# Second products of four experts with the model's columns on the partitions, turned back through memory

## The chip, the cores and the metric

The kernel runs on one core of a Trainium2 chip. The metric is the device time of one execution in microseconds (us), shown as the median of three runs.

## What is computed

The program is a linear-recurrence attention followed by a mixture of eight experts with the best two experts for each token. Only the experts matter here. For N = 3072 tokens of D = 384 numbers, E = 8 experts and F = 1024 hidden columns:

```python
out = np.zeros((N, D), dtype=np.float32)
for e in range(E):
    for k in range(2):
        mask = top2[:, k] == e
        h = np.maximum(x[mask] @ w1[e], 0.0)
        out[mask] += top2_w[mask, k, None] * (h @ w2[e])
```

## The kernel before, in words

The tokens of an expert lie in a table in memory, with room for up to 832 of them. Experts 2 to 7 are taken in the order of their token counts (`rank`, `EX`), so each position in the loop at L1193 has a fixed number of rows: `REST` (L347) gives 64, 64, 64, 48, 32, 16, 16 and 0 for positions 0 to 7. "Expert e" below is the e-th in this order. Its rows come in two pieces. The first piece (`w == 0`) has 256 + REST[e] rows, in row tiles 0, 1 (128 rows each) and 2 (REST[e] rows). The second piece (`w == 1`) has 512 rows, in tiles 3 to 6.

Every float32 factor is split into two parts, a high part and the remainder (`split`, `h`, `x`), and every product is the sum of three: high times high, high times low, low times high. TensorE therefore does three matmuls for each block.

An expert is worked off in this order (L1197 to L1216):

- `load_w2` (L841): four DMAs on SP's queue bring the second weights into the three buffers `raw`; ScalarE casts the high part (L829), VectorE subtracts for the low part (L830).
- `gather_o` (L904): GpSimd gathers the rows of `out` that belong to the expert's tokens into the tiles `ao`.
- `mm1` (L883) for both pieces: for each of eight blocks f of hidden columns, nine matmuls of 128 stationary columns (of W1) and n moving columns (the tokens), into one of four PSUM banks `ph`. ScalarE applies the ReLU (L898), VectorE forms the low part (L901). In the first piece VectorE does that in two instructions, since the remainder's rows are laid out apart, beside a padded gap that GpSimd clears (L892).
- in between, SP loads the next expert's tokens (`load_x`) and first weights (`load_w1`). `x_P` (L789) splits the tokens' 32-bit words into two planes of 16 bits (ScalarE, L794) in the tiles `xp0` and `xp1` and writes them to memory, and `x_L` (L798) reads them back with twelve transposing DMAs (L803).
- `mm2` (L914) for the first piece: for each full row tile 24 matmuls with 128 columns of h stationary and the 384 columns of W2 moving, into one of two banks `po`. For tile 2, eight matmuls whose stationary operand holds high and low rows side by side (L927) and eight more (L930); ScalarE copies the low half out (L933) and VectorE adds it (L934). After each tile VectorE adds the gated result to `ao` (L935, `kept`) and GpSimd scatters `ao` into `out` (L936).
- `mm2` for the second piece, tile by tile, and after the tiles the planes of the next expert are put together (`x_T`, L865): VectorE copies the planes into one tile `xj` (L877), which has a single buffer, ScalarE casts (L880), VectorE subtracts (L881). A manual edge keeps each such copy behind the last `kept` before it.

What orders the work: the engines run their queues in order. Up to the end of expert 1 the order is written out by hand (`ORDER`). From expert 2 on a planner fills each engine's queue. It prefers what stands earlier in the program, and takes a later instruction when the earlier one isn't ready by its own reckoning. On SP a callback (`queue`, L1186) chains all DMAs of this loop in program order:

```python
    def queue(ins):
        if ENG.get(ins.engine) == "SP" and not type(ins).__name__.startswith(("Bass", "InstRegister")):
            if loads:
                tc.add_manual_dep(ins, loads[-1].name, after, reason="order")
            loads.append(ins)
```

Of the kernel before, what the change touches and what calls it, by code (L numbers as in the profile page):

```python
# [9 lines left out]
F32 = mybir.dt.float32  # L10
# [3 lines left out]
U16 = mybir.dt.uint16  # L14
I32 = mybir.dt.int32
AF = mybir.ActivationFunctionType
OP = mybir.AluOpType
# [302 lines left out]
def kernel(  # L320
# [8 lines left out]
    nc = tc.nc  # L329
# [5 lines left out]
    N, DM = out.shape  # L335
    E = w_gate.shape[1]
    FF = w1.shape[2]
    KD = DM // 128
    KF = FF // 128
# [6 lines left out]
    G0 = 3  # L346
    REST = (64, 64, 64, 48, 32, 16, 16, 0)  # L347
    JS = ((0, 1, 2), (3, 4, 5, 6))
    TO = (0, 128, 256, 0, 128, 256, 384)

    def width(e, w):
        return 256 + REST[e] if w == 0 else 512

    def tile_rows(e, j):
        return REST[e] if j == 2 else 128

    def tiles_of(e, w):
        return [j for j in JS[w] if tile_rows(e, j)]

    def pad(e):  # L360
        return -(-REST[e] // 32) * 32
# [3 lines left out]
    xs = nc.dram_tensor("xs", [E * N, ROW], F32, kind="Internal").ap()  # L365
    es = nc.dram_tensor("es", [NT, HD], F32, kind="Internal").ap()
    xp = nc.dram_tensor("xp", [2, 7 * 128, 2 * DM], U16, kind="Internal").ap()
    xd = nc.dram_tensor("xd", [N, DM + E], F32, kind="Internal").ap()

    cp = ctx.enter_context(tc.tile_pool(name="cp", bufs=1))  # L370
# [39 lines left out]
    none = cp.tile([128, ROW], F32, name="none")  # L410
# [14 lines left out]
    ap = ctx.enter_context(ExitStack())  # L425
# [361 lines left out]
    after = mybir.DependencyInfo(mybir.DependencyClass.NoSync, mybir.DependencyReason.DATA)  # L787

    def x_P(e, w):  # L789
        js = JS[w]  # L790
        src_t = (xga, xgb)[w]
# [6 lines left out]
    def x_L(e, w):  # L798
        lo, n = JS[w][0] * 128, width(e, w)
        for kk in range(KD):  # L800
# [11 lines left out]
    W1, W2, XW, HT, GW, OX = {}, {}, {}, {}, {}, {}  # L812
    where = {}

    def mt(shape, dt, name, **kw):

        return where.setdefault(name, mpools[-1]).tile(shape, dt, name=name, **kw)
# [9 lines left out]
    order = mybir.DependencyInfo(mybir.DependencyClass.NoSync, mybir.DependencyReason.DATA)  # L827
# [13 lines left out]
    def load_w2(e):  # L841
        for f2 in range(KF // 2):
            r = mt([128, FF], F32, name="raw", bufs=RAW)
            rv = r[:, :2 * DM].rearrange("p (f d) -> p f d", f=2)
            nc.sync.dma_start(rv, of(w2, e)[f2 * 256:(f2 + 1) * 256, :].rearrange("(f p) d -> p f d", p=128))
            W2[f2] = [mt([128, 2, DM], F32R, name=f"w2{x}{f2}") for x in "hl"]
            split(rv, *W2[f2])
# [17 lines left out]
    def x_T(e, w, kk):  # L865
        n = width(e, w)
        src_t = xga if w == 0 else xgb
        js = JS[w]
        x = XW[w, kk] = mt([128, 2, width(0, w)], F32R, name=f"x{w}{kk}")[:, :, 0:n]
        if e < 2:  # L870
            p = ps_tile("px")
            for j in js:
                o = TO[j]
                nc.tensor.transpose(p[:, o:o + 128], src_t[:, j - js[0], kk * 128:(kk + 1) * 128], ident)
        else:
            p = mt([128, 512], F32, name="xj")
            t = nc.vector.tensor_copy(p[:, :n].bitcast(U16).rearrange("p (d two) -> p two d", two=2), XU[w, kk])  # L877
            if e > 2:
                tc.add_manual_dep(t.ins, kept[-1].ins.name, after, reason="order")
        nc.scalar.copy(x[:, 0, :], p[:, :n])  # L880
        nc.vector.tensor_tensor(x[:, 1, :], p[:, :n], x[:, 0, :].bitcast(F32), op=OP.subtract)  # L881

    def mm1(e, w, fs=range(KF)):  # L883
        n = width(e, w)
        for f in fs:

            h = mt([128, 2 * width(0, w)], F32R, name=f"h{w}{f}")
            t, u = (REST[e], pad(e)) if w == 0 else (0, 0)
            m = n - t + u
            HT[w, f] = h[:, 0:m + t], h[:, m + t:]  # L890
            if u > t:
                nc.gpsimd.memset(h[:, n:m].bitcast(F32), 0.0)  # L892
            p = ps_tile("ph", 4)
            ms = [(i, j, kk) for kk in range(KD) for i, j in ((0, 0), (0, 1), (1, 0))]
            for c, (i, j, kk) in enumerate(ms):
                nc.tensor.matmul(p[:, :n], W1[e, kk][i][:, f * 128:(f + 1) * 128], XW[w, kk][:, j, :],  # L896
                                 start=(c == 0), stop=(c == len(ms) - 1))
            nc.scalar.activation(h[:, 0:n], p[:, :n], AF.Relu)  # L898
            for dst, a, b in ((m + t, 0, n - t), (m, n - t, n)):
                if a < b:  # L900
                    nc.vector.scalar_tensor_tensor(h[:, dst:dst + b - a], p[:, a:b], 0.0, h[:, a:b].bitcast(F32),  # L901
                                                   op0=OP.max, op1=OP.subtract)

    def gather_o(e):  # L904
        for j in tiles_of(e, 0) + tiles_of(e, 1):
            w = tile_rows(e, j)
            nc.gpsimd.indirect_dma_start(  # L907
                out=ao[j][0:w, :], out_offset=None, in_=out,
                in_offset=bass.IndirectOffsetOnAxis(ap=OX[e][0:w, j:j + 1], axis=0),
                bounds_check=N - 1, oob_is_err=False)  # L910

    osc, kept = {}, []

    def mm2(e, w, js=None):  # L914
        for j in js or tiles_of(e, w):
            n, o, u = tile_rows(e, j), TO[j], pad(e)
            p = psO.tile([128, 512], F32, name="po")
            a, g = ao[j][0:n, :], GW[e][0:n, j:j + 1]
            if n == 128:
                ms = [(f, i, k2) for f in range(KF) for i, k2 in ((0, 0), (0, 1), (1, 0))]  # L920
                for m, (f, i, k2) in enumerate(ms):
                    nc.tensor.matmul(p[:, :DM], HT[w, f][i][:, o:o + 128], W2[f // 2][k2][:, f % 2, :],  # L922
                                     start=(m == 0), stop=(m == len(ms) - 1))
            else:

                for f in range(KF):
                    nc.tensor.matmul(p[0:u + n, :DM], HT[w, f][0][:, o:o + u + n], W2[f // 2][0][:, f % 2, :],  # L927
                                     start=(f == 0), stop=(f == KF - 1), skip_group_check=True)
                for f in range(KF):
                    nc.tensor.matmul(p[0:n, :DM], HT[w, f][0][:, o:o + n], W2[f // 2][1][:, f % 2, :],  # L930
                                     start=False, stop=(f == KF - 1), skip_group_check=True)
                lo = mt([64, DM], F32, name="lo")[0:n]
                nc.scalar.copy(lo, p[u:u + n, :DM])  # L933
                nc.vector.scalar_tensor_tensor(a, lo, g, a, op0=OP.mult, op1=OP.add)  # L934
            kept.append(nc.vector.scalar_tensor_tensor(a, p[0:n, :DM], g, a, op0=OP.mult, op1=OP.add))  # L935
            d = nc.gpsimd.indirect_dma_start(  # L936
                out=out, out_offset=bass.IndirectOffsetOnAxis(ap=OX[e][0:n, j:j + 1], axis=0),
                in_=a, in_offset=None, bounds_check=N - 1, oob_is_err=False)
            for x in osc.setdefault(e, []):
                tc.declare_no_dep(d.ins, x.ins, reason="tokens differ")  # L940
            osc[e].append(d)


    P = dict(la=10, p1=7, d1=1, p2=6, dt=0, ds=0, lqk=6, p3=4, d3=0, q=2, lv=4, xu=0.5, ss=3, gl=0, gd=0.25,
             tr=1.4, sc=-0.2, st=0.05, y=0.2, up=0.4, w1=18, w2=21.1, xt=18.5, m1=19.1, dm=0.26, xu1=22.8, w1b=23, co=6, hg=50,
# [2 lines left out]
    for g in range(NG):  # L948
        f = B * g + .5
        q1, q2, q3 = P.get(f"s{g}", (P["p1"], P["p2"], P["p3"]))  # L950
        for j in range(B // 2):
            m = B * g // 2 + j
            h = phase_of(m) // 2
            i = [x for x in range(m + 1) if phase_of(x) == 2 * h].index(m)
# [6 lines left out]
        for j in range(B):  # L961
            n = B * g + j
# [123 lines left out]
    psO = mctx.enter_context(tc.tile_pool(name="psO", bufs=2, space=PSUM, reuse_waits="tile"))  # L1086
    psB.append(mctx.enter_context(tc.tile_pool(name="psB", bufs=2, space=PSUM, reuse_waits="tile")))
    ao = [mp.tile([128, DM], F32, name=f"ao{j}") for j in range(7)]
# [49 lines left out]
    for e, tokens in ORDER.items():  # L1138
        tokens = tokens.split()
# [53 lines left out]
    for e in range(2, E):  # L1193
        if e == 3:
            flag = flags()
            held.close()
        load_w2(e)  # L1197
        gather_o(e)
        mm1(e, 0)
        if e + 1 < E:  # L1200
            load_x(e + 1, 0, xga)
            load_x(e + 1, 1, xgb)
        mm1(e, 1)
        if e + 1 < E:
            load_w1(e + 1)
            for w in range(2):
                x_G(e + 1, w)
                x_P(e + 1, w)
            for w in range(2):
                x_L(e + 1, w)  # L1210
        mm2(e, 0)
        for j in JS[1]:
            mm2(e, 1, (j,))
            if e + 1 < E:
                for w, kk in {3: ((0, 0), (0, 1)), 4: ((0, 2), (1, 0)), 5: ((1, 1),), 6: ((1, 2),)}[j]:
                    x_T(e + 1, w, kk)  # L1216
    nc.pop_inst_callback()
    mctx.close()

# [168 lines left out]
```

## Time and profile before

| what | value |
|---|---|
| median of 3 runs | 675.37 us (674.38 to 676.07) |
| the profiled execution's own time | 675.33 us |
| its span, first to last instruction | 673.6 us |
| TensorE busy | 655.4 us (97%) |
| VectorE, ScalarE, GpSimd busy | 433.4, 357.6, 181.6 us |
| mean granted TensorE clock | 0.997 of full speed |

The profiled execution took 1.7 us more than its span, and 0.04 us less than the median. Experts 3 to 7 fill the last 272 us of it. Busy shares are means over the whole span, so what a change to one stage is worth has to be read from that stage's rows.

### The profile page before, as it was taken

To read this page: it belongs to the slowest core of one execution; us is meant where nothing else is said; L and a number is where in the kernel's file an instruction comes from. 1 tells how busy PE (TensorE), PEld (TensorE's weight loads), DVE (VectorE), ACT (ScalarE), POOL (GpSimd) and SP (SyncE) were. 2 spreads that over 40 slices of the span, in tenths; PEclk is the share of its full clock that TensorE was granted. 3 is DMA by queue.
4 is the path that set the end of the run, shared out by engine and by line. 5 is a ranking of instruction groups with operands and counts; after the bars stand their busy time and mean duration, and the time that the engine had idled before them with its cause. 6 is when DMAs were issued, how large, how long until landed. Compare 5 with 4: busy or idle time off the path is not lost.

```text
span 673.6 us, 14401 instructions
## 1 busy us (share of the span) xinstructions
PE 655.4 (97%) x5516; PEld 578.1 (86%) x5519; DVE 433.4 (64%) x998; ACT 357.6 (53%) x596; POOL 181.6 (27%) x209
## 2 busy tenths in 40 slices
PE   7999999999999999999999999999999999999995
PEld 3467787888888999898998998999999899899895
DVE  7899999999998666435467266258247437527311
ACT  6899999999855543425137137128118316504200
POOL 3000000154555340034333224124222331423211
PEclk9999999999999999999999999999999999999998
DMA  6765756678499535265727548718737846642101
GB/s 235 225 210 145 226 146 220 202 217 258 126 283 320 193 129 206 65 210 159 214 93 280 122 164 279 159 67 284 150 115 251 167 127 228 186 139 68 57 36 35
DMA packets 100220, 117.85 MB, mean 175 GB/s; under 512 B 57338, under 2 KB 79307, under 8 KB 100144
## 3 DMA queue, kind: packets, MB, share of 16 engines
q1 hardware_dynamic: 90816, 89.32, 44.1%
q0 software_dynamic: 9328, 27.54, 12.8%
q8 instruction: 45, 0.74, 0.5%
q14 instruction: 31, 0.25, 0.1%
HBM read 70.26 MB, written 40.02 MB: 164 GB/s over the span
## 4 chain that ended last, share of the span: by engine, by line
PE 78%; ACT 9%; DVE 6%; DMA 3%; issue 2%; SPq 0%; POOL 0%; POOLq 0%; ACTq 0%
PE ph L896 29%; PE po L922 29%; PE ptr L577 3%; PE psc L587 3%; ACT t L461 2%; PE pY L636 2%; PE pY L638 2%; PE psc L896 2%; PE po L930 1%; PE po L927 1%; PE cum L554 1%; ACT L460 1%; PE pG L599 1%; PE cum L646 1%; DMA re<-in_a_dram 1%
## 5 line engine op out<-in xcount | busy, mean ns | idle before, releaser
L922 PE MATMUL po<-w2h,h 128*128 128x384 f32 x768 | 198.6, 335 | 0.0
L896 PE MATMUL ph<-x,w1h 128*128 128x512 f32 (+5 forms) x720 | 186.6, 347 | 0.0
L922 PEld LDWEIGHTS po<-w2h,h 128*128 128x128 f32 x768 | 139.0, 188 | 1.0 <-DVE h L901 0.3
L896 PEld LDWEIGHTS ph<-x,w1h 128*128 128x128 f32 x720 | 125.8, 188 | 14.8 <-DVE x L881 0.4
L922 PE MATMUL po<-w2l,h 128*128 128x384 f32 x384 | 128.5, 335 | 0.0
L896 PE MATMUL ph<-x,w1l 128*128 128x512 f32 (+5 forms) x360 | 124.7, 346 | 0.1
L936 POOL DMA_INDIRECT out_dram<-ao,ox x55 | 57.9, 1053 | 246.2 <-DVE ao L935 205.6
L901 DVE SCALAR_TENSOR_TENSOR h<-ph,h 128x512 fp32r<-128x512 f32 (+5 forms) x168 | 71.2, 455 | 79.6 <-ACT h L898 78.0
L898 ACT ACTIVATE h<-ph 128x512 fp32r<-128x512 f32 (+5 forms) x120 | 60.8, 513 | 97.5 <-PE ph L896 87.1
L711 POOL DMA_INDIRECT xs<-xr,sl x48 | 59.5, 1239 | 176.5 <-DVE ga4mx L299 126.0
L935 DVE SCALAR_TENSOR_TENSOR ao<-po,gw,ao 128x384 f32<-128x384 f32 (+4 forms) x55 | 33.7, 613 | 78.3 <-PE po L922 77.2
L896 PEld LDWEIGHTS ph<-x,w1l 128*128 128x128 f32 x360 | 67.7, 188 | 7.9 <-DVE w1l L830 0.4
L922 PEld LDWEIGHTS po<-w2l,h 128*128 128x128 f32 x384 | 72.1, 188 | 0.4
L907 POOL DMA_INDIRECT ao<-out_dram,ox x48 | 54.3, 1132 | 52.1 <-issue 41.8
L880 ACT CAST x<-xj 128x512 fp32r<-128x512 f32 (+5 forms) x36 | 18.9, 525 | 63.8 <-DVE xj L877 63.8
L587 PE MATMUL psc<-qT,kT 112*64 112x128 f32 (+1 forms) x768 | 39.3, 249 | 1.1 <-DVE am L588 0.8
L587 PEld LDWEIGHTS psc<-qT,kT 112*64 112x64 f32 x768 | 35.9, 137 | 4.5 <-ACT kT L578 2.6
L638 PE MATMUL pY<-am,v 128*48 128x128 f32 x384 | 35.6, 273 | 0.3 <-ACT xT L639 0.3
L830 DVE TENSOR_TENSOR w2l<-raw,w2h 128x768 fp32r<-128x768 f32 x32 | 30.1, 951 | 7.3 <-ACT w2h L829 7.2
L829 ACT CAST w2h<-raw 128x768 fp32r<-128x768 f32 x32 | 26.2, 835 | 14.4 <-PE po L922 8.5
L588 DVE TENSOR_TENSOR am<-psc,mask 128x512 f32<-128x512 f32 x48 | 32.0, 681 | 2.6 <-PE psc L587 2.4
L830 DVE TENSOR_TENSOR w1l<-raw,w1h 128x1024 fp32r<-128x1024 f32 x24 | 29.2, 1220 | 4.4 <-ACT w1h L829 4.3
(229 smaller groups left out, 1000.3 us busy)
## 6 DMA issues: line engine op xcount, KB each, us to landing
raw<-in_moe_w_dram SPq DMA_DIRECT2D x24, 512.0 KB
raw<-in_moe_w_dram SPq DMA_DIRECT2D x32, 384.0 KB
qk<-in_qk_dram SPq DMA_DIRECT2D x24, 384.0 KB
v<-in_v_dram SPq DMA_DIRECT2D x24, 288.0 KB
xgb<-xs SPq DMA_DIRECT2D x8, 800.0 KB
re<-in_a_dram SPq DMA_DIRECT2D x12, 384.0 KB
im<-in_a_dram SPq DMA_DIRECT2D x12, 384.0 KB
out_dram<-none SPq DMA_DIRECT2D x12, 384.0 KB
```

What stands on the lines that cost most here:

```text
L587: nc.tensor.matmul(p[o:o + 64, j, z:], KT[n][:, h, z:z + 64], QT[n][:, h, z:], start=True, stop=True, skip_group_check=True)
L588: nc.vector.tensor_mul(AM[n][:, 4 * half:4 * half + 4, :].rearrange("p (a r) t -> p a (r t)", r=2), p.rearrange("p (a r) t -> p a (r t)", ...
L638: nc.tensor.matmul(o, V[n][:, H + h // 2 if h % 2 else h, :], AM[n][:, h, :], start=not g, stop=True, skip_group_check=True)
L711: d = nc.gpsimd.indirect_dma_start(out=xs, out_offset=bass.IndirectOffsetOnAxis(ap=sl[:, kk, b:b + 1], axis=0), in_=XR[g][:, lo + b, :], i ...
L830: nc.vector.tensor_tensor(lo, raw_t, hi.bitcast(F32), op=OP.subtract)
L896: nc.tensor.matmul(p[:, :n], W1[e, kk][i][:, f * 128:(f + 1) * 128], XW[w, kk][:, j, :], start=(c == 0), stop=(c == len(ms) - 1))
L898: nc.scalar.activation(h[:, 0:n], p[:, :n], AF.Relu)
L901: nc.vector.scalar_tensor_tensor(h[:, dst:dst + b - a], p[:, a:b], 0.0, h[:, a:b].bitcast(F32), op0=OP.max, op1=OP.subtract)
L907: nc.gpsimd.indirect_dma_start(out=ao[j][0:w, :], out_offset=None, in_=out, in_offset=bass.IndirectOffsetOnAxis(ap=OX[e][0:w, j:j + 1], ax ...
L922: nc.tensor.matmul(p[:, :DM], HT[w, f][i][:, o:o + 128], W2[f // 2][k2][:, f % 2, :], start=(m == 0), stop=(m == len(ms) - 1))
L935: kept.append(nc.vector.scalar_tensor_tensor(a, p[0:n, :DM], g, a, op0=OP.mult, op1=OP.add))
L936: d = nc.gpsimd.indirect_dma_start(out=out, out_offset=bass.IndirectOffsetOnAxis(ap=OX[e][0:n, j:j + 1], axis=0), in_=a, in_offset=None, b ...
```

## The change

For the experts in `FLIP` (3 to 6) the second products of the first piece exchange their operands. W2's columns become the stationary operand, in three blocks of 128 (kk), and the tokens move: 24 matmuls of n = 256 + REST[e] columns for each block, 72 in all, where there were 48 and 16. The result has the model's columns on the partitions. ScalarE copies each block out of PSUM as two planes of 16 bits into the tile `xp0`, SP writes it to a table `op` in memory (three DMAs), and two transposing DMAs bring the two planes back into `xp1`, with the tokens on the partitions. After the second piece's tiles VectorE puts the planes of each row tile together in `xj`, adds the gated result to `ao`, and GpSimd scatters it. The side-by-side layout of h goes for these experts, and with it the clearing of the gap and the second VectorE instruction for each block. Once, at expert 2, two DMAs clear the columns 256 to 383 of `op`.

```diff
+    FLIP = (3, 4, 5, 6)
...
+    op = nc.dram_tensor("op", [2, 2, DM, 3 * 128], U16, kind="Internal").ap()
...
-            t, u = (REST[e], pad(e)) if w == 0 else (0, 0)
-            m = n - t + u
+            t, u = (REST[e], pad(e)) if w == 0 and e not in FLIP else (0, 0)
+            m = n - t + u if t else width(0, w)
...
+    def send_o(e, j, a):
...
+    def mm2_turned(e):
+        n = width(e, 0)
+        t = mt([128, len(JS[0]), 2, DM], U16, name="xp0").rearrange("p a b c -> p (a b c)")[:, 0:KD * 2 * n]
+        t = t.rearrange("p (k two n) -> p k two n", k=KD, two=2)
+        for kk in range(KD):
+            p = psO.tile([128, 512], F32, name="po")
+            ms = [(f, i, k2) for f in range(KF) for i, k2 in ((0, 0), (0, 1), (1, 0))]
+            for m, (f, i, k2) in enumerate(ms):
+                nc.tensor.matmul(p[:, :n], W2[f // 2][k2][:, f % 2, kk * 128:(kk + 1) * 128], HT[0, f][i][:, 0:n],
+                                 start=(m == 0), stop=(m == len(ms) - 1))
+            nc.scalar.copy(t[:, kk], p[:, :n].bitcast(U16).rearrange("p (d two) -> p two d", two=2))
+            nc.sync.dma_start(op[e % 2, :, kk * 128:(kk + 1) * 128, 0:n].rearrange("two p n -> p two n"), t[:, kk])
+
+    def turn_back(e):
+        y = mt([128, len(JS[1]), 2, DM], U16, name="xp1").rearrange("p a b c -> p (a b c)")[:, 0:6 * DM]
+        y = y.rearrange("p (two j d) -> p two j d", two=2, j=3)
+        for i in range(2):
+            nc.sync.dma_start(y[:, i], op[e % 2, i], transpose=True)
+        return y
+
+    def add_turned(e, y):
+        for j in tiles_of(e, 0):
+            n = tile_rows(e, j)
+            x = mt([128, 512], F32, name="xj")[0:n, :DM]
+            t = nc.vector.tensor_copy(x.bitcast(U16).rearrange("p (d two) -> p two d", two=2), y[0:n, :, j])
+            tc.add_manual_dep(t.ins, kept[-1].ins.name, after, reason="order")
+            a, g = ao[j][0:n, :], GW[e][0:n, j:j + 1]
+            nc.vector.scalar_tensor_tensor(a, x, g, a, op0=OP.mult, op1=OP.add)
+            send_o(e, j, a)
...
         load_w2(e)
+        if e == 2:
+            for i in range(2):
+                nc.sync.dma_start(op[i, :, :, 256:384].rearrange("two (k p) n -> p (two k) n", p=128),
+                                  none.bitcast(U16)[:, None, 0:128].to_broadcast([128, 2 * KD, 128]))
         gather_o(e)
...
-        mm2(e, 0)
+        if e in FLIP:
+            mm2_turned(e)
+            y = turn_back(e)
+        else:
+            mm2(e, 0)
         for j in JS[1]:
             mm2(e, 1, (j,))
...
+        if e in FLIP:
+            add_turned(e, y)
```

`send_o` is the scatter that stood at the end of `mm2`, unchanged, as a function.

## Rows read from the trace of the kernel before

**Rows 1.** The page: span, and busy time of each engine.
```profile
span 673.6 us, 14401 instructions
## 1 busy us (share of the span) xinstructions
PE 655.4 (97%) x5516; PEld 578.1 (86%) x5519; DVE 433.4 (64%) x998; ACT 357.6 (53%) x596; POOL 181.6 (27%) x209
```

**Rows 2.** Stretches of TensorE: from:to, length, busy (matmuls), clock, DMA share, GB/s.
```profile
401.15:411.19 10.04, 10.04 (x75) 1.00 0.95 324
...
427.54:438.69 11.15, 11.15 (x65) 1.00 0.66 185
438.69:455.35 16.66, 16.66 (x97) 1.00 0.14 50
455.35:464.83 9.48, 9.48 (x73) 1.00 0.99 356
481.18:492.29 11.11, 11.11 (x65) 1.00 0.66 185
508.93:518.01 9.08, 9.08 (x74) 1.00 0.95 323
534.38:545.54 11.16, 11.16 (x65) 1.00 0.61 155
```

**Rows 3.** Groups of VectorE's instructions by form, from 395 us on.
```profile
L935 DVE SCALAR_TENSOR_TENSOR ao<-po,gw,ao 128x384 f32<-128x384 f32 x32 | 19.7, 616 | 57.8 <-PE po L922 57.7
L830 DVE TENSOR_TENSOR w2l<-raw,w2h 128x768 fp32r<-128x768 f32 x20 | 19.0, 950 | 3.0 <-ACT w2h L829 3.0
...
L877 DVE COPY xj<-xu 128x1024 uint16<-128x1024 uint16 x15 | 11.3, 751 | 0.2
...
L877 DVE COPY xj<-xu 128x544 uint16<-128x544 uint16 x6 | 2.8, 474 | 0.1
...
L901 DVE SCALAR_TENSOR_TENSOR h<-ph,h 128x16 fp32r<-128x16 f32 x16 | 2.6, 163 | 0.0
```

**Rows 4.** Groups of ScalarE's instructions by form, from 395 us on.
```profile
L794 ACT COPY xp<-xga 128x768 uint16<-128x768 uint16 x12 | 9.9, 830 | 1.0 <-DMA xga<-xs 1.0
```

**Rows 5.** SP's queue: transposes of 470 to 487 us, timeline, and its longest such wait.
```profile
L803 SPq DMA_TRANSPOSE xu<-xp x6: 1242/1242/1924, 470.4 to 477.5; - x6
...
L803 SPq DMA_TRANSPOSE xu<-xp x7: 1242/1259/1262, 477.5 to 485.3; - x7
...
470.38 16.18 SPq L803 DMA_TRANSPOSE xu<-xp  x12
486.80 21.48 SPq L845 DMA_DIRECT2D raw<-in_moe_w_dram  x4
...
SPq L803 <- DMA xp<-xp: 4.2, 1, 4.2
```

**Rows 6.** VectorE in order of time, from expert 4 to expert 5.
```profile
509.80 0.76 DVE L877 COPY xj<-xu 128x1024 uint16<-128x1024 uint16 x1
...
511.29 0.69 DVE L881 TENSOR_TENSOR x<-xj,x 128x512 fp32r<-128x512 f32 x1
511.90 0.42 DVE L901 SCALAR_TENSOR_TENSOR h<-ph,h 128x256 fp32r<-128x256 f32 x1
512.24 0.95 DVE L830 TENSOR_TENSOR w2l<-raw,w2h 128x768 fp32r<-128x768 f32 x1
513.10 0.99 DVE L901 SCALAR_TENSOR_TENSOR h<-ph,h 128x16 fp32r<-128x16 f32 x5
...
514.85 0.17 DVE L861 TENSOR_TENSOR order<-xga,order 128x18 f32<-128x18 f32 x1
514.93 0.16 DVE L863 CAST ox<-xga 128x3 uint32<-128x3 f32 x1
515.05 0.17 DVE L862 TENSOR_REDUCE gw<-order 128x3 f32<-128x18 f32 x1
```

**Rows 7.** ScalarE in order of time, the first cast of expert 5's second weights.
```profile
506.06 0.83 ACT L829 CAST w2h<-raw 128x768 fp32r<-128x768 f32 x1 [1.76 <-PE po L922]
```

**Rows 8.** GpSimd's last gather for expert 7, and VectorE's first use of such a row.
```profile
627.25 1.00 POOL L907 DMA_INDIRECT ao<-out_dram,ox  x1 [0.30 <-issue]
...
644.89 0.62 DVE L935 SCALAR_TENSOR_TENSOR ao<-po,gw,ao 128x384 f32<-128x384 f32 x1 [2.80 <-PE po L922]
```

More of the change, by code (lines that the diff above doesn't have):

```diff
@@ L912 @@
     osc, kept = {}, []
+    def send_o(e, j, a):
+        n = tile_rows(e, j)
+        d = nc.gpsimd.indirect_dma_start(
+            out=out, out_offset=bass.IndirectOffsetOnAxis(ap=OX[e][0:n, j:j + 1], axis=0),
+            in_=a, in_offset=None, bounds_check=N - 1, oob_is_err=False)
+        for x in osc.setdefault(e, []):
+            tc.declare_no_dep(d.ins, x.ins, reason="tokens differ")
+        osc[e].append(d)
     def mm2(e, w, js=None):
@@ L935, in mm2 @@
             kept.append(nc.vector.scalar_tensor_tensor(a, p[0:n, :DM], g, a, op0=OP.mult, op1=OP.add))
[L936 to L941, printed above, removed]
+            send_o(e, j, a)
[19 more added lines that the diff above has]
+        for j in tiles_of(e, 0):
+            n = tile_rows(e, j)
+            x = mt([128, 512], F32, name="xj")[0:n, :DM]
[3 more added lines that the diff above has]
+            nc.vector.scalar_tensor_tensor(a, x, g, a, op0=OP.mult, op1=OP.add)
+            send_o(e, j, a)
     P = dict(la=10, p1=7, d1=1, p2=6, dt=0, ds=0, lqk=6, p3=4, d3=0, q=2, lv=4, xu=0.5, ss=3, gl=0, gd=0.25,
```

## The prediction

> **What bounds the kernel now.** I read the page first. TensorE is busy for 655.4 of 673.6 us [rows 1], so the question for any other engine is whether it makes TensorE wait. The stretches of TensorE show the last five experts without a gap: busy time equals length in each, at full clock [rows 2]. There a matmul that goes away is time that goes away, and a wait that TensorE gets is time added. Two shapes stand side by side in these rows. The first products of a first piece are 72 matmuls with 128 stationary and 304, 288 or 272 moving columns: 10.04, 9.48 and 9.08 us, or 139, 132 and 126 ns each. The second products of a first piece are 64 matmuls with 384 moving columns: 11.15, 11.11 and 11.16 us, or 174 ns each [rows 2]. (Some counts are one to three off, by matmuls that straddle a stretch's edge or belong to the flags.) So the step follows the moving columns.
>
> **TensorE's saving.** The turned products are 72 matmuls with the shape of the first products: the same 128 stationary columns, the same n moving ones, the same three-part pattern. I price them by those rows: expert 3 goes from 11.15 to 10.04 (saves 1.11), expert 4 from 11.11 to 9.48 (1.63), expert 5 from 11.16 to 9.08 (2.08) [rows 2]. Expert 6 has expert 5's shapes: 2.08. Sum **6.90 us**. A rule speaks against this: the Trainium skill's page "TensorE: Matmul & The Clock Gate", section "Back-to-back issue gap", gives streams of weight load and matmul a step of about 81 ns at 128 columns and 131 ns at 512, so only about 0.13 ns per column. By it (an estimate, on a line between the two) 64 steps at 384 columns and 72 at 272 to 304 cost about the same, and the saving would be near zero. The rows have 126 against 174 ns for 272 against 384 columns, 0.43 ns per column, so here the trace disagrees with that rule.
>
> **What moves on VectorE.** Three gated additions (L935) and one more (L934) leave the stage of the first piece. Behind the last tile come three copies of 768 16-bit elements and three gated additions. The same copy takes 0.474 us for 544 and 0.751 for 1024 elements [rows 3]: 0.60 by interpolation. The addition takes 0.62 [rows 3]. That is 3 x 1.22 = 3.66 us, put exactly where VectorE is late: expert 5's first products begin at 508.93, and there VectorE still does the last `x_T` copy (509.80) and subtraction (511.29), reaches the first low part of h at 511.90 and finishes it in the group begun at 513.10 [rows 6]. TensorE has four banks; its fifth group starts at 508.93 + 4 x 1.135 = 513.47 and needs that low part. Its slack is a few tenths, so this edit isn't free. In relief, for experts 4 to 6 the second small piece of each low part (0.16 us, eight per expert) goes [rows 3].
>
> Two orders bound the price. If the six new instructions run as one block behind the subtraction, they end at 511.98 + 3.66 = 515.6, the first low part at 516.1, and TensorE waits 2.6 us. If a low part slips in after the first copy, it ends at 511.98 + 0.60 + 0.43 = 513.0 and nothing waits; if both the last weight subtraction (0.95) and the addition (0.62) go ahead of it, it ends at 514.6 and TensorE waits 1.1. The new six hang on each other, each on the one before, through `xj`'s single buffer. The queue shows what the planner does with such pairs: the reduction L862 needs L861, and the independent L863 stands between them [rows 6]. A chain of six leaves five such places. I take the interleaved order, 0.3 us at each of the four handovers (3 to 4, up to 6 to 7): **1.2 us**, with ends of nothing and 10.4. Less than nothing is excluded, since TensorE had no gap there to give back.
>
> **What moves on SP.** Three writes and two transposes for each flipped expert stand ahead of the next expert's second weights. In expert 4 the twelve transposes end at 486.6 [rows 5]. The turned products would run from 481.18 to 490.66, the third ScalarE copy (up to 0.83 us for 768 elements; here 576 [rows 4]) ends by 491.5, and the write goes out. SP then waits for it to land. The one time that the trace shows SP waiting for a write before reading it back, it was 4.2 us [rows 5]; I take that, with nothing as the low end: 496 us. Of a 384 by 384 transpose there is no row. Those of 288 and 512 rows by 128 columns cost SP 1.24 and 1.26 us [rows 5], so rows are nearly free; with three blocks of columns the bounds are 1.25 and 3 x 1.26 = 3.8 us each. I take the low one, since the cost didn't grow with data: SP is free at 498.5, at 503.6 by the high end.
>
> Two consumers follow. VectorE wants the planes 3.05 us after the second piece, which by rows 2 and 6 lasts 16.64 us: 490.66 + 16.6 + 3.05 = 510.3. That cover of 7 to 12 us hides the landing. Without it, every microsecond of lateness is one of VectorE standing in line, with the low parts of h behind it, and beyond about half a microsecond one of TensorE. The second weights were issued at 486.80 before [rows 5] and would be at 498.5 to 503.6. ScalarE's first cast began at 506.06 [rows 7]; 1.6 us of saving earlier that is 504.4. A 384 KB load at the 324 GB/s of a full stage [rows 2] takes 1.2 us, plus 4.2 for landing: 503.9 at the low end, just in time, 509.0 at the high.
>
> The landing has a second price. The Trainium skill's page "DMA: Bandwidth & Descriptors", section "Anatomy of one DMA", puts the fixed cost at about 2.0 us, mostly the receipt of the last byte. By it write and load would each be 2.2 us earlier and the second weights' lateness gone from nearly all of the interval. No row here separates receipt from data.
>
> **Edits that cost nothing while covered.** Three ScalarE copies replace one; each bank is read while the other fills for over 3 us, and if that cover went the price would be 0.83 us each. Eight GpSimd clearings go; no row above waits for them. Three scatters come behind the last tile, about 6 us later than now, and the next gathers queue behind them on GpSimd. Expert 7's last gather is issued by 628.3 and its first row is used at 644.9 [rows 8]: 16 us of cover. The two clearing DMAs at expert 2 cost SP two issues once, at most 3.8 us each, ahead of loads for the next expert; TensorE's next need of those is a whole expert away.
>
> **Sum.** The profiled execution took 675.33 us, 1.7 more than its span and 0.04 less than the median, which I neglect. 675.33 - 6.90 + 1.2 = **669.6 us**. With waits of 0 to 1.1 us at each handover the forecast's own range is 668.4 to 672.8.
>
> **Rivals.**
> A, slower: the block. The planner finds the planes ready and runs the six at once, h behind them; it decides once the block plus one low part passes the fifth group's start, 1.5 us behind the subtraction. 675.33 - 6.90 + 4 x 2.6 = 678.8 us. For it: the six stand earlier in the program than h. Against: the slipped-in L863 [rows 6]. A part of it, waits of 1.1 to 2.0 us each, gives 672.8 to 676.4.
> B, SP: transposes at the high end, so ScalarE's casts start up to 4.6 us late with the ReLUs behind them. The fifth group starts 4.5 us into the stage and the first group needs 1.2 of that for itself, so 3.3 are covered; 1.3 us each remain: 675.33 - 6.90 + 5.2 = 673.6 us. Against it: the flat cost with size.
> C: a transpose costs SP 1.25 us for each of its nine blocks. Two take 22.5 us, the planes come at 518.5 plus landing, 12 us late: 4 x 12 more, 716 us. Against it: the 512-row transposes hold four blocks and cost 1.26 [rows 5].
> D: the step doesn't follow the columns and nothing is saved: 675.3 us. That is a mechanism of this kernel only if rows 2 mislead; the page named above is its reason.
>
> **Chances.** Forecast 0.62, A 0.13, part of A 0.08, B 0.10, C 0.03, D 0.02, and 0.02 for a saving with no wait at all, 668.4. A difference under 0.3% (2.0 us) can't be told from none here. Faster: the forecast, the 0.02, half of part-A, and 0.04 of B: 0.72. Same: the other half, the rest of B, and D: 0.12. Slower: A and C: 0.16. The range runs from 667.6, the full saving less the spread of runs (0.8), to 675.6, above part of A and B; A and C stay out.
>
> **What would show it.** Right: 72 matmuls per flipped expert in 10.0, 9.5, 9.1 and 9.1 us; the low parts of h between the new copies and additions; idle time before TensorE's fifth group under 1.1 us; two transposes under 4 us of SP each; the planes landed before VectorE asks. Wrong: six new VectorE instructions without one between (A), ScalarE's casts waiting for `raw` (B), VectorE waiting for the planes (C), a step of 174 ns (D).

## The result, and the profile after

The changed kernel took **669.93 us** (median of 6 runs, 668.44 to 670.81), beside 675.56 us (674.38 to 678.09) for the kernel before in the same series: ratio 0.9912, interval 0.9891 to 0.9934. The forecast was 669.6 us. The profiled execution shown here took 670.81 us, 0.9 above that median, so its sum is made against the 675.33 us of the profiled execution before: 4.52 us less.

The page, its first lines; they answer to [rows 1]:

```profile
span 668.8 us, 14343 instructions
## 1 busy us (share of the span) xinstructions
PE 649.0 (97%) x5551; PEld 574.2 (86%) x5551; DVE 432.8 (65%) x974; ACT 364.0 (54%) x604; POOL 175.8 (26%) x185
```

TensorE executes more matmuls in less time. The stretches of TensorE, with the columns of [rows 2]: for experts 3 to 6 the second products of the first piece, now turned (first, fourth, sixth and eighth row), one second piece (second row), and the first products of the next expert's first piece (the others):

```profile
427.68:437.60 9.92, 9.92 (x73) 1.00 0.40 97
437.60:454.27 16.67, 16.67 (x99) 1.00 0.61 150
454.27:463.75 9.48, 9.48 (x74) 1.00 1.00 353
480.09:489.56 9.47, 9.47 (x73) 1.00 0.61 107
506.23:517.10 10.87, 9.29 (x74) 1.00 0.98 336
533.43:542.46 9.03, 9.03 (x74) 1.00 0.69 163
559.11:568.23 9.12, 9.12 (x73) 1.00 0.93 323
584.59:593.62 9.03, 9.03 (x74) 1.00 0.64 112
610.27:619.22 8.95, 8.95 (x75) 1.00 0.29 101
```

Against [rows 2] the turned stages save 1.23, 1.64, 2.13 and 2.13 (expert 6's stage took 11.16 before as well): 7.13 us. Only one row has a length above its busy time: expert 5's first products, 10.87 where [rows 2] have 9.08. (The 8.95 of expert 7 holds 0.23 us of its own second products, put forward by the planner.) So 7.13 is gained and 1.79 given back in one place, the handover from expert 4 to expert 5: 675.33 - 7.13 + 1.79 = 669.99. Of the 0.8 us up to 670.81, 0.3 lies around the span (2.0 us, 1.7 before), 0.1 ahead of expert 3, 0.1 in expert 7's stages, and 0.3 behind TensorE's last matmul (8.3 us to the end of the span, 8.0 before). The waits of TensorE name the 1.79 (total, times, longest). TensorE in order of time shows it ahead of the sixth group of nine matmuls; the fifth began on time, 4.52 us into the stage:

```profile
PE ph L898 <- DVE h L903: 1.6, 1, 1.6
```
```profile
511.74 0.29 PE L898 MATMUL ph<-x,w1l 128*128 128x272 f32 x1
513.61 0.52 PE L898 MATMUL ph<-x,w1h 128*128 128x272 f32 x2 [1.58 <-DVE h L903]
```

VectorE in order of time at that handover (compare [rows 6]; L974 is the copy of a turned tile, L977 its gated addition, L903 the low part of h, L832 the subtraction for a second-weight tile):

```profile
508.55 0.68 DVE L883 TENSOR_TENSOR x<-xj,x 128x512 fp32r<-128x512 f32 x1
509.15 0.43 DVE L903 SCALAR_TENSOR_TENSOR h<-ph,h 128x272 fp32r<-128x272 f32 x1
509.50 0.60 DVE L974 COPY xj<-xp 128x768 uint16<-128x768 uint16 x1
511.72 0.96 DVE L832 TENSOR_TENSOR w2l<-raw,w2h 128x768 fp32r<-128x768 f32 x1 [1.62 <-ACT w2h L831]
512.59 0.61 DVE L977 SCALAR_TENSOR_TENSOR ao<-xj,gw,ao 128x384 f32<-128x384 f32 x1
513.12 0.43 DVE L903 SCALAR_TENSOR_TENSOR h<-ph,h 128x272 fp32r<-128x272 f32 x1
513.47 0.65 DVE L974 COPY xj<-xp 128x768 uint16<-128x768 uint16 x1
514.02 0.42 DVE L903 SCALAR_TENSOR_TENSOR h<-ph,h 128x272 fp32r<-128x272 f32 x1
```

The new six stand one at a time between the low parts, no block. But VectorE stood idle for 1.62 us in front of a subtraction, and the second low part of h was queued behind it. ScalarE in order of time says why: the cast of the fourth second-weight tile waited for its load, which SP had issued at 505.16.

```profile
507.55 0.40 ACT L900 ACTIVATE h<-ph 128x272 fp32r<-128x272 f32 x1 [1.33 <-PE ph L898]
510.85 0.84 ACT L831 CAST w2h<-raw 128x768 fp32r<-128x768 f32 x1 [2.39 <-DMA raw<-in_moe_w_dram]
511.59 0.39 ACT L900 ACTIVATE h<-ph 128x272 fp32r<-128x272 f32 x1
```

The second low part would have been ready in time but for that load: at the handover from 5 to 6 VectorE has the same order with the load on time, and the sixth group (second row) follows without a wait.

```profile
564.26 0.44 DVE L903 SCALAR_TENSOR_TENSOR h<-ph,h 128x272 fp32r<-128x272 f32 x1
564.75 0.52 PE L898 MATMUL ph<-x,w1h 128*128 128x272 f32 x2
```

Before, the same load was issued at 507.91 and its cast began at 511.17 without a wait, 3.26 us later; here it was 5.69 us. SP's queue itself was early (expert 4; the last row counts all eight transposes, with minimum, median and maximum in ns):

```profile
488.21 2.59 SPq L961 DMA_DIRECT2D op<-xp  x3
492.46 2.78 SPq L967 DMA_TRANSPOSE xp<-op  x2
495.49 10.04 SPq L847 DMA_DIRECT2D raw<-in_moe_w_dram  x4
```
```profile
L967 SPq DMA_TRANSPOSE xp<-op x8: 1304/1375/2302, 440.5 to 597.8; - x8
```

SP is free at 495.24, and no VectorE instruction ever waits for the planes.

### The profile page after: what moved, and what is told of

The parts are those of the page before. It is cut to its first block, busy times and chain, and to the rows that moved or that the text cites. A ratio compares the mean times of both kernels' runs of the same rounds, so it can differ in the third digit from the quotient of the medians.

```text
span 668.8 us, 14343 instructions
## 1 busy us (share of the span) xinstructions
PE 649.0 (97%) x5551; PEld 574.2 (86%) x5551; DVE 432.8 (65%) x974; ACT 364.0 (54%) x604; POOL 175.8 (26%) x185
## 4 chain that ended last, share of the span: by engine, by line
PE 74%; ACT 9%; DVE 7%; DMA 5%; issue 2%; SPq 1%; POOL 0%; POOLq 0%; ACTq 0%
PE ph L898 29%; PE po L933 23%; PE po L958 6%; PE ptr L579 3%; PE psc L589 2%; ACT t L463 2%; PE pY L638 2%; PE pY L640 2%; PE psc L898 2%; ACT ee L463 2%; PE cum L556 1%; DMA xs<-xr,sl 1%; DMA raw<-in_moe_w_dram 1%; ACT qT L580 1%; ACT L462 1%
## 5 line engine op out<-in xcount | busy, mean ns | idle before, releaser
L933 PE MATMUL po<-w2h,h 128*128 128x384 f32 x640 | 165.2, 335 | 0.0
L918 POOL DMA_INDIRECT out_dram<-ao,ox x55 | 59.6, 1084 | 255.4 <-DVE ao L946 195.8
L903 DVE SCALAR_TENSOR_TENSOR h<-ph,h 128x512 fp32r<-128x512 f32 (+5 forms) x136 | 69.6, 528 | 73.6 <-ACT h L900 73.3
L933 PEld LDWEIGHTS po<-w2h,h 128*128 128x128 f32 x640 | 115.8, 188 | 0.6 <-DVE h L903 0.3
L933 PE MATMUL po<-w2l,h 128*128 128x384 f32 x320 | 107.0, 334 | 0.0
L946 DVE SCALAR_TENSOR_TENSOR ao<-po,gw,ao 128x384 f32<-128x384 f32 (+1 forms) x43 | 26.3, 612 | 92.2 <-PE po L933 91.7
L909 POOL DMA_INDIRECT ao<-out_dram,ox x48 | 50.4, 1050 | 43.1 <-issue 34.2
L933 PEld LDWEIGHTS po<-w2l,h 128*128 128x128 f32 x320 | 60.1, 188 | 0.2
L958 PE MATMUL po<-h,w2h 128*128 128x272 f32 (+2 forms) x192 | 38.1, 292 | 0.0
L832 DVE TENSOR_TENSOR w2l<-raw,w2h 128x768 fp32r<-128x768 f32 x32 | 30.1, 952 | 9.5 <-ACT w2h L831 9.4
```

The costliest lines, as they stand in the source:

```text
L832: nc.vector.tensor_tensor(lo, raw_t, hi.bitcast(F32), op=OP.subtract)
L909: nc.gpsimd.indirect_dma_start(out=ao[j][0:w, :], out_offset=None, in_=out, in_offset=bass.IndirectOffsetOnAxis(ap=OX[e][0:w, j:j + 1], ax ...
L918: d = nc.gpsimd.indirect_dma_start(out=out, out_offset=bass.IndirectOffsetOnAxis(ap=OX[e][0:n, j:j + 1], axis=0), in_=a, in_offset=None, b ...
L958: nc.tensor.matmul(p[:, :n], W2[f // 2][k2][:, f % 2, kk * 128:(kk + 1) * 128], HT[0, f][i][:, 0:n], start=(m == 0), stop=(m == len(ms) - 1))
```

## Experiments

Three theories. **T**: TensorE's saving stands; the price is what VectorE has in line ahead of the low parts at a handover. **S**: SP and its transposes are late, and the second weights with them. **L**: one load lands late, whatever VectorE does. Diffs are against the changed kernel. Line numbers shift by a few where code is added.

**1. The six as one block** (rival A made real): each low part of a first piece is ordered behind the last turned addition.

```diff
+                    if w == 0 and e - 1 in FLIP:
+                        tc.add_manual_dep(d.ins, added[-1].ins.name, after, reason="order")
```

> Every low part of h of the next expert's first piece is kept behind the last of the six new VectorE instructions, so that they run as one block; nothing else differs from the changed kernel. My account (the interleaving is what keeps TensorE busy): TensorE waits about 2.6 us at each of the four handovers, so some 8 to 10 us more than the changed kernel's 669.9: 677 to 680 us, slower than before. The rival (the four banks and the slow second piece absorb VectorE's lateness): 669 to 671 us.

Measured: 690.64 us, ratio 1.0204 (1.0176 to 1.0232), far above both. TensorE's waits, then its stretches at the handover from expert 4 to 5:

```profile
PE ph L898 <- DVE h L903: 15.6, 4, 4.8
```
```profile
511.42:516.20 4.78, 4.78 (x40) 1.00 0.88 272
516.20:521.38 5.18, 0.40 (x5) 0.74 0.97 386
521.38:524.00 2.62, 2.62 (x11) 0.50 1.02 395
524.00:527.82 3.82, 3.82 (x27) 0.81 0.08 31
```

The order is worth some 21 us, so the interleaving is what makes this change pay. Three things were not in the price of 2.6 us for each handover. At three handovers the planner also put the next tokens' small operations (L863 to L865) into the block, and at two of them one waited for its load, 0.72 and 1.44 us. At the handover from 4 to 5 VectorE stood 1.83 us ahead of the block for the late load. So the waits were 2.9 to 4.8 us. And after a wait the granted clock fell: 0.50 in the third row (that is 1.2 GHz of 2.4), where a matmul took 2.62 / 11 = 0.24 us instead of 4.78 / 40 = 0.12. The handover cost 16.40 where it takes 9.08; 0.5 of the 7.3 us are four second products put forward (their own stage takes 8.52 instead of 9.03), so 6.8 us were lost for a wait of 4.8. In the changed kernel the wait of 1.58 us left the clock at 1.00.

**2. No turned additions.** Left out: the copies, gated additions and scatters of the turned results, so four experts' first pieces are missing from the output.

```diff
-        if e in FLIP:
-            add_turned(e, y)
```

> Leaves out the putting together, the gated additions and the scatters of the turned results (the first pieces of experts 3 to 6 are missing from the output); matmuls, plane copies, writes and transposes stay. If VectorE's six instructions cause the remaining waits (2.1 us in the changed kernel's profile, my forecast had 1.2): 668.2 to 669.2 us, and no wait of TensorE for a low part of h. Rival: the waits come from the fourth load of the second weights, which lands late and holds up ScalarE; then they stay and the time is within 0.5 us of 669.9.

Measured: 667.77 us, ratio 0.9873 (0.9853 to 0.9893). Expert 5's first products take 9.03 us, so the wait is gone, and the time is below the range of either theory. But ScalarE waited only 0.59 us for the fourth load in this profile, which costs next to nothing even with the six in line (0.52 us cost 0.04 in the table below), so the run doesn't tell T from L. All that stands behind the last tiles is worth 669.93 - 667.77 = 2.2 us, and the rest of the turn (copies out, writes, transposes) costs nothing that can be seen: the saving alone gives 675.56 - 7.13 = 668.4, no less.

**3. The additions later**: the turned tiles of expert e - 1 are added, and the rows of expert e gathered, behind `mm1(e, 0)`.

```diff
-        gather_o(e)
-        mm1(e, 0)
+        if e - 1 in FLIP:
+            mm1(e, 0)
+            add_turned(e - 1, y)
+            gather_o(e)
```

> The same work, but the six VectorE instructions and the scatters stand behind the next expert's first products of the first piece in the program, and the gathers behind them. My account: the small waits behind VectorE go, 668.4 to 669.5 us. Rival: the tile that holds the planes is then free later, the next expert's planes are split later, and ScalarE or the SP queue makes TensorE wait: 670.5 us or more.

Measured: 669.06 us, ratio 0.9895 (0.9876 to 0.9913); expert 5's first products 9.30 us. T's size, but not cleanly: ScalarE waited only 1.34 us for the fourth load in this profile. So it was run again, beside the changed kernel:

> The changed kernel once more, unedited, beside the version with the additions moved. Both theories expect 669.5 to 670.5 us here, and in the profile a wait of 1.5 to 2 us in the first products of expert 5 alone.

> The additions of the turned products issued behind the next expert's first products, run again beside the changed kernel. If the six VectorE instructions at the handover are what TensorE waits for, it is 0.7 to 1.5 us faster than the changed kernel in the same call, at 668.3 to 669.4 us, and the first products of expert 5 take under 9.4 us. If the wait is the late fourth load of the second weights alone, it is within 0.3 us of the changed kernel.

Measured: 669.67 us for the changed kernel (ratio 0.9913, 0.9898 to 0.9928) and 668.78 us for the edit (0.9895, 0.9879 to 0.9911). The intervals overlap; over both series the means are 669.70 (12 runs) and 668.87 (11 runs), 0.84 us apart with a standard error of 0.30. It is the best complete version found. Expert 5's first products missed both expectations: the changed kernel's lost 1.0 us in this profile, not 1.5 to 2, and the edit's took 9.80 us, not under 9.4. First the changed kernel's row, then the edit's:

```profile
505.94:516.04 10.10, 9.30 (x73) 1.00 0.88 296
```
```profile
506.82:516.62 9.80, 9.29 (x73) 1.00 0.95 330
```

**4. More transposes.** First each transpose issued three times onto the same tile; then, since such repeats wait for each other, one extra pair into a tile nobody reads.

```diff
-            nc.sync.dma_start(y[:, i], op[e % 2, i], transpose=True)
+            for _ in range(3):
+                nc.sync.dma_start(y[:, i], op[e % 2, i], transpose=True)
```

> Each transpose is issued three times, six where there were two; the result is the same. SP is held about 5.6 us longer ahead of the second weights' loads (two transposes take 2.8 us of it in the changed kernel's profile), and the planes land 5 to 6 us later. My account: both stay covered, or nearly; at most 1 us at each handover: 669.5 to 673 us. Rival B of the prediction (the second weights' lateness comes through to TensorE): 1.3 us or more at each, 675 us and up; if the planes' lateness came through, VectorE would wait for them.

Measured: 704.95 us, ratio 1.0448 (1.0414 to 1.0481). SP's queue at expert 3, and the waits of ScalarE, VectorE and TensorE:

```profile
439.98 17.86 SPq L968 DMA_TRANSPOSE xp<-op  x6
458.05 6.20 SPq L847 DMA_DIRECT2D raw<-in_moe_w_dram  x4
```
```profile
ACT w2h L831 <- DMA raw<-in_moe_w_dram: 36.9, 10, 6.3
DVE xj L975 <- DMA xp<-op: 12.9, 4, 3.7
PE po L958 <- ACT w2h L831: 10.1, 3, 3.6
```

This is S as a fact: with SP at the second weights at 458.05 instead of 444.42, both waits that rivals B and C named appear. The edit costs far more than its six issues, because each repeat waits for the one before to land.

```diff
+        z = mt([128, len(JS[0]), 2, DM], U16, name="xp0").rearrange("p a b c -> p (a b c)")[:, 0:6 * DM]
+        z = z.rearrange("p (two j d) -> p two j d", two=2, j=3)
+        for i in range(2):
+            nc.sync.dma_start(z[:, i], op[e % 2, i], transpose=True)
```

> Behind the two transposes stand two more of the same size into another tile that nothing reads, so that none waits for another to land (the run with six had each repeat wait for the one before it on the same tile, which held SP nearly 18 us instead of 8). SP reaches the second weights' loads about 2.8 us later. My account: the three early loads land by about 501 us in the changed kernel where ScalarE asks at 503.3, so most of 2.8 us is covered: 669.5 to 672 us. Rival: the queue is already without cover, and 2.8 us at each of four handovers come through at the rate of the run with six: 675 us or more.

Measured: 672.63 us, ratio 0.9966 (0.994 to 0.9992). Confounded: the extra tile is `xp0`, and at one handover ScalarE's copy of the next tokens waited 4.91 us for it, with the casts of expert 6's tokens behind it and VectorE 3.83 us behind those. The first products of experts 4 to 7 took 10.01, 10.18, 11.65 and 8.94 us, where the changed kernel's two profiles have 9.48, 10.10 to 10.87, 9.12 and 8.95. So some 3 us more of SP cost 0.5 us at one handover and nothing at two, and the loss at the handover from 5 to 6 stands beside that copy: with its queue as it is in the changed kernel, SP isn't what TensorE waits for.

**5. One buffer tile for the four loads**, to issue the fourth early.

```diff
-            r = mt([128, FF], F32, name="raw", bufs=RAW)
-            rv = r[:, :2 * DM].rearrange("p (f d) -> p f d", f=2)
+            rv = raws()[:, f2 * 2 * DM:(f2 + 1) * 2 * DM].rearrange("p (f d) -> p f d", f=2)
```

(`load_w1` likewise; `raws()` is one tile of `RAW` times 1024 columns.)

> The three buffers of 4 KB for raw weights become one tile of 12 KB, in which the four second-weight loads of 3 KB each have their own place; the fourth no longer waits for the first to be split, and no longer holds the SP queue. If the remaining waits of TensorE at the handover come from the late fourth load (ScalarE waited 2.4 us for it in the changed kernel's profile, then VectorE, then TensorE 1.6): 667.8 to 669.2 us and no such wait. Rival (VectorE's six instructions alone make TensorE wait): within 0.5 us of 669.9.

Measured: 695.03 us, ratio 1.0275 (1.0251 to 1.0299). Inconclusive: the planner made another order, in which VectorE stood 15.17 us for token loads at expert 2 and TensorE 10.4 behind it. It shows how much an order can cost here, nothing on the load.

**6. Which experts are turned.** `FLIP` is (2, 3, 4, 5, 6), (5, 6) or (3, 4).

```diff
-    FLIP = (3, 4, 5, 6)
+    FLIP = (5, 6)
```

> Expert 2 is turned as well, with 320 tokens. If TensorE's step goes by the moving columns: 72 matmuls at 147 ns (10.6 us) for 11.1 us, 0.5 us saved, less what the handover from 2 to 3 costs (0 to 0.6): 669.2 to 670.3 us. Rival (a step that doesn't follow the columns): the stage of expert 2 takes 9 to 10 us.

> Only experts 5 and 6 are turned. Each stage goes from 11.16 to 9.03 us as in the changed kernel's profile, 4.26 us together, less a wait of 0.3 at the last handover: 671.2 to 672.0 us. If the waits seen at the handover from 4 to 5 come with the flip of expert 4, they are gone here. Rival: the saving per expert is an average of something else, and half the experts give half of 5.6: 672.7 us or more.

> Only experts 3 and 4 turned. The saving on TensorE is 1.23 + 1.64 = 2.87 us. If the handover from expert 4 to 5 costs its 1.8 us whenever expert 4 is turned, the time is 675.5 - 2.9 + 1.8 = 674.4 us (673.8 to 674.9), and the first products of expert 5 take 10.5 to 11 us. If that wait needs something later in the program, or is a matter of one profile, 672.4 to 673.2 us and 9.1 to 9.4 us.

Measured: 671.09 us (0.9925, 0.9905 to 0.9946), 670.54 us (0.9924, 0.9903 to 0.9945) and 672.92 us (0.9961, 0.9946 to 0.9976). A fifth expert brings nothing that can be measured, and its time is 0.8 us above the expected range: its second products fall from 11.40 to 10.91 us, and at its own handover expert 3's two stages of first products grow by 0.36 and 0.70. With (5, 6) the handover from 4 to 5 costs nothing (second row), and the turned stages save their 2.13 each; the 4.9 us from this series' 675.48 are 0.7 more than that, though expert 4's first products, ahead of any turned expert, even took 0.48 longer than in [rows 2] (first row). I can't say where the rest comes from. (Where expert 3's first products begin differs between profiles by up to 1.5 us, from 400.36 to 401.89, through work far ahead of the change; stages are therefore compared by their own lengths.) With (3, 4) the saving is 675.20 - 672.92 = 2.3 us, below the 2.87 of the two stages: neither theory's stage time came, since the planner put some of expert 5's second products into its first (third and fourth rows), but together the two take 21.35 us against 9.08 + 11.16 [rows 2], 1.11 more. In order: (5, 6), two rows, then (3, 4), two rows.

```profile
455.00:464.96 9.96, 9.64 (x73) 1.00 0.98 344
509.18:518.20 9.02, 9.02 (x74) 1.00 0.99 335
```
```profile
505.29:517.05 11.76, 11.07 (x82) 1.00 0.97 346
533.40:542.99 9.59, 9.59 (x57) 1.00 0.68 181
```

**7. The token loads out of the way.** At the handover from 4 to 5 alone, the next expert's tokens are loaded behind its first weights, so that SP issues nothing but two first-weight loads while the late load is under way.

```diff
-        if e + 1 < E:
+        if e + 1 < E and e != 5:
             load_x(e + 1, 0, xga)
             load_x(e + 1, 1, xgb)
...
             load_w1(e + 1)
+            if e == 5:
+                load_x(e + 1, 0, xga)
+                load_x(e + 1, 1, xgb)
```

> At the handover from expert 4 to 5 alone, SP issues the next expert's token loads behind its first weights instead of right behind the fourth load of the second weights. VectorE's order up to the last low part of the first piece is that of the changed kernel. If the fourth load lands late because the token loads share its time, it lands within 3.3 us of its issue, as at the other handovers, ScalarE's cast of it does not wait, the first products of expert 5 take 9.0 to 9.4 us, and the time is 668.0 to 669.0 us. If it is late for another reason, ScalarE still waits 0.5 to 2.4 us there, those products take 9.8 to 10.9 us, and the time is 669.4 to 670.4 us.

Measured: 670.51 us, ratio 0.992 (0.9901 to 0.9938). Contention with the token loads is not the cause: the load issued at 505.69 was still late, and its stage took 10.48 us.

```profile
510.99 0.83 ACT L831 CAST w2h<-raw 128x768 fp32r<-128x768 f32 x1 [2.00 <-DMA raw<-in_moe_w_dram]
```

## Why the prediction was right, step by step

The number was within 0.4 us, in part by luck: the saving came out somewhat larger than forecast, VectorE's term far smaller, and a late load that the sum didn't have took what they left.

**TensorE's saving**: 6.90 predicted, 7.13 measured. The turned stages took 9.92, 9.47, 9.03 and 9.03 us, each 0.01 to 0.12 under the first products whose shape they have. Rival D is out: 72 matmuls of 272 columns are 125 ns each and 64 of 384 were 174 [rows 2]. The trace disagrees again with the rule of the Trainium skill's page "TensorE: Matmul & The Clock Gate", section "Back-to-back issue gap", by which they would be some 100 and 114 ns (an estimate, on a line between its two figures).

**VectorE, 0.3 us at each of four handovers**: the sum was near (1.2 predicted; 1.8 to 1.9 in the profile shown, 1.1 in the second profile), the account behind it wrong. The six are interleaved, as predicted, but three handovers cost at most 0.1 us and one costs 1.0 to 1.8. The step that failed is which low part TensorE waits for. The prediction put the first low part behind the first copy or later, with the fifth group needing it and a slack of "a few tenths". In the rows the first low part (509.15) stands ahead of all six and the fifth group never waits. The copy, the last weight subtraction and the addition, which were to cost 1.1 us ahead of the first low part, stand ahead of the second, which is needed by the sixth group only, 1.13 us later; with the loads on time that costs 0.1 us at most. The rest comes with the fourth weight tile, which the prediction took to be on time. In eleven profiles the handover from 4 to 5 reads as follows; a dash marks the one where the stages are mixed (1.11 from the sum above):

| kernel | cast waits for the fourth load, us | first products of expert 5, us | above 9.08 |
|---|---|---|---|
| before | 0 | 9.08 | 0 |
| experts 5, 6 only | 0 | 9.02 | 0 |
| experts 2 to 6 | 0.52 | 9.12 | 0.04 |
| changed, second profile | 1.61 | 10.10 | 1.02 |
| two more transposes | 1.68 | 10.18 | 1.10 |
| experts 3, 4 only | 1.73 | - | 1.11 |
| token loads late | 2.00 | 10.48 | 1.40 |
| changed, first profile | 2.39 | 10.87 | 1.79 |
| no additions | 0.59 | 9.03 | 0 |
| additions later, first | 1.34 | 9.30 | 0.22 |
| additions later, second | 1.84 | 9.80 | 0.72 |

With the six in line, TensorE's loss is the lateness less 0.6 us, in each of the five rows with a loss over 0.1. With the six behind the first products it is the lateness less 1.12, in two rows. So the six cost 0.5 us there, and the VectorE rows show which 0.5: one gated addition (L977, from 512.59 to 513.12) ahead of the low part. Without lateness it is covered, but barely: at the handover from 5 to 6 the second low part ends at 564.70 and the sixth group begins at 564.75. T and L both hold, each for its part; moving the additions saves 0.5 here, 0.1 at each of the next two.

**SP**: the write was priced at 4.2 us for landing; the third write is issued at 490.43 and the transposes begin at 492.46, so it had landed within 2.0 us (4.2 was another write, [rows 5]). The Trainium skill's page "DMA: Bandwidth & Descriptors", section "Anatomy of one DMA", which I cited with about 2.0 us, was nearer than my row. That section is about DMAs that GpSimd issues, and this write is SP's, so the agreement doesn't test it. The transposes cost SP a median of 1.375 us, near the low bound of 1.25 and flat with the blocks: rivals B and C fall on price, and experiment 4 shows that their mechanism was real. SP was free 3.3 us earlier than forecast, 1.1 of them by expert 3's saving, which the forecast had not carried into expert 4's times. The second weights were late all the same, by a load that landed slowly and not by a queue that issued late, which no rival had.

**Rival A** fell as argued, by the interleaving. Its price was far too low: 690.64 us measured, 678.8 given. The sum left out the small operations that join a block, the loads waited for, and the clock.

**Covered edits**: the planes were copied out in 0.61 to 0.67 us each (up to 0.83 allowed), and neither VectorE nor TensorE waited for the gathers or for the scatters behind the tiles.

## What to carry to other kernels

Where TensorE is without a gap, a product can be priced by the nearest row of its own shape, and exchanging operands so that fewer columns move is worth that difference. What the exchange pushes behind the tiles should be ordered behind the next stage's feeding work, or between it piece by piece: as one block it cost some 21 us here. When one stage alone loses time, compare issue and landing of every transfer that it uses across several profiles before blaming the instructions added.

## What was not expected of the hardware

**One load of 384 KB took 3.8 to 5.7 us from its issue to its cast where its like took 3.4 at most, and always beside the same thing.** The DMA view lists a queue q8 of the kind "instruction". In the changed kernel, over the whole span (packets, MB, share):

```profile
q8 instruction: 45, 0.74, 0.5%
```

That is 16 KB in a packet, or one for some 247 of TensorE's 11102 matmuls and weight loads, whose instructions they may be; the trace doesn't say whose. In the changed kernel one came at 507 to 508, while the late load was under way, and in the kernel before at 512 to 513, after that load was in (the rows of these two stretches of 1 us, in this order; 10.1% of 16 engines is one engine for 1.6 us):

```profile
q8 instruction: 1, 0.02, 10.1%
```
```profile
q8 instruction: 1, 0.02, 6.0%
```

I looked at the fourth second-weight load at all four handovers of twelve profiles, 48 loads (the runs with six transposes and with one buffer tile are left out, since all their loads come at other times). In ten, a q8 packet came 0.9 to 2.5 us after the issue, and in just these ten ScalarE waited, 0.5 to 2.4 us; all ten are the handover from 4 to 5 of kernels in which expert 4 is turned. Among the 38 others, with no packet or one 2.9 us or more after the issue, none was waited for by more than 0.1 us.

The single packets and landings in the traces show how. Such a load goes as 256 packets of 1.5 KB, and its landing is told in 16 steps, so a step stands for the 16 packets of one DMA engine. In all ten late loads 15 steps came within 3.3 us of the issue, and the last one alone 3.8 to 5.7 us after it. In eight of the ten the last 16 packets began within 0.02 us of the end of the q8 packet. In the changed kernel the load was issued at 505.16, the q8 packet took from 507.31 to 508.93, 16 packets of the load ran from 508.92 to 510.37, and the last step came at 510.83. So one engine held its whole share of the load back until it was through with the instruction packet, and the lateness goes by when that packet ends: in nine of the ten the last step came 1.9 to 2.0 us after it, in the tenth 1.5.

What puts the packet there is a reading: turning experts 3 and 4 adds 16 matmuls, and 16 weight loads, ahead of it. No run here moved the packet alone.

**A wait of 1.6 us left TensorE's clock at 1.00; after each of the four waits of 2.9 to 4.8 us in experiment 1 it was granted 0.50 for a while.** That made the handover shown there cost 6.8 us for a wait of 4.8.

**The order of the queues is a size of its own.** Two small edits that add no work cost 21 and 25 us by their order, which experiment 1 imposed and the planner made in experiment 5.
